# Raw weight pieces in left places, lo parts on VectorE, theta of tiles 0 to 9 in attention: one change to a fused recurrence, mixing and transform kernel

## The chip, the cores and the metric

The kernel runs on one core of one Trainium2 chip. The metric is the device time of one execution in microseconds (us), as the median of several runs. The engines are TensorE (PE in the rows, PEld its weight loads), VectorE (DVE), ScalarE (ACT), GpSimd (POOL) and the SyncE queue that issues most transfers (SP).

## What is computed

Three stages follow one another on 4 batches of 768 tokens with 384 channels (8 heads of 48). The reference, cut to what matters:

```
# 1 attention: a recurrence with decay w and bonus u
cur   = k_t v_t^T * u ;  y_t = r_t (state + cur) ;  state = w_t * state + k_t v_t^T
# 2 mixing over tokens and channels, x is attention's y
theta = x @ w_theta
zr, zi = x * cos(theta), x * sin(theta)
y = w_tok_r @ zr + w_tok_i @ zi          # over the 768 tokens, for every batch
u = x + y ;  x = u + relu(u @ w_ch)
# 3 transform and feed-forward
u = x + real(fft(fft(x, tokens), channels))
out = u + relu(norm(u) @ w_ch1) @ w_ch2
```

The weights arrive as 64-bit floating point numbers, and are made into 32-bit ones on the chip.

## The kernel before

**Weights.** `Feed` loads a weight in pieces of 128 rows. A piece is loaded raw (two 32-bit words for each number, 768 KB for a piece of 768 columns) by `issue`, and `convert` makes one f32 tile of it: ScalarE scales the high words (L496, `prescale`), then VectorE runs three bit operations (L511, L514, L517). There are two raw buffers, so a new raw load can start only when an older piece has been converted. Pieces come in a fixed order: two for w_theta, then twelve for the token weights (w_tok_r and w_tok_i in turn, parts 0 to 11; token tile j needs parts 2j and 2j+1), two for w_ch, and twelve for the feed-forward weights, which go back to DRAM (`store`) after conversion and are read again later. Attention converts the two pieces of w_theta and parts 0 to 5; part 0 goes through DRAM (`tx`), parts 1 to 5 are put into `tst` tiles in the places T19 to T23. The rest is converted in the mixing stage.

**Exact products.** A product of f32 accuracy is made of three matmuls (`mm3`, L445 to L447): each operand is split into a rounded "hi" part and the rest, "lo". The hi part is a copy on ScalarE (L451), the lo part a subtraction (L452) on VectorE or GpSimd, as `split` is told. For the token weights from tile 1 on, for w_ch, and for one of the two z tiles (L651) it is GpSimd before.

**Attention** runs over 16 pairs of heads (i = 0 to 15, four for a batch) in a software pipeline: `front(i)` (transposes L213, products L221, diagonals on ScalarE L228), then `elem` for a later tile on VectorE or some weight conversions (`pieces`: one at i = 1, 5, 9 and 15, two at 13 and 14), then `front2(i)` (copy under a mask L251, L268, the scan L273) and `back(i - 1)` (products L290 and L295, copies of the result out of PSUM L298, stores L305). `THETAS` says at which i the theta matmuls (L433) of which 128-token tiles run in the banks that `back` uses; the result goes to DRAM (L197). At i = 16, which has only a `back`, two more are computed before. Each engine works its instructions off in program order.

**Mixing** (`dense`) is a generator: attention calls `next(nxt)` for its first parts, and the rest follows. It runs over 24 tiles (n = 0 to 23, six for a batch). In loop n TensorE transposes tile n+1 (`tokens`, L610) and then runs the 36 matmuls of tile n (`tok_half`, twice); meanwhile VectorE and ScalarE make tile n+1: turns of theta (L632 to L634), sines (L640, L641), products with x (L646, L647), hi parts (L648, L649) and lo parts (L651, L652). Conversions of pieces are put between these by `side` from the list `work`. Theta of a tile is read back from DRAM if it is in `STORED` or `AHEAD` (`fetch`, L622), else computed in the loop (`angle`). The four tiles of `AHEAD` are computed in loops 0 to 3 and stored. After the sixth tile of a batch come `add_x` and `chan`, the channel product, whose operand u is split by ScalarE and GpSimd. Behind n = 23 follows the last stage, which the change does not touch.

## Time and profile before

| what | value |
|---|---|
| runs | 804.67, 809.67, 808.92 us, median 808.92 us |
| profiled execution | 804.06 us, its span 802.2 us |
| attention | 0 to about 178 us of the span |
| mixing | about 165 to 430 us |
| feed-forward stage | about 430 to 802 us |
| TensorE busy | 744.0 us, 93% |
| VectorE, ScalarE, GpSimd busy | 522.1, 310.7, 173.8 us |

The span runs from the first to the last instruction. Shares are averages over stages with different limits: in the last stage TensorE runs almost without a gap, while around 130 to 265 us it has gaps, and in some of these slices its granted clock is below full speed.

### The profile page before, as it was taken

Reading aid. Unit: us, or ns where it says so; the run is one execution under the profiler, and the core shown is the slowest. Engines: PE = TensorE matmul, PEld = TensorE weight load, DVE = VectorE, ACT = ScalarE, POOL = GpSimd, SP = SyncE. Lnnn points to the kernel's source line nnn. Section 1 sums busy time; section 2 is a strip of 40 time slices with the busy share of each in tenths; the row PEclk is TensorE's granted clock in tenths of the full one; section 3 lists DMA queues with packets and bytes.
Section 4 is the critical chain, followed back from the end, with each engine's and each line's share of the span. In section 5 each row is a group of like instructions: output and inputs, shape, how many; then the busy total and the mean of one; then the engine's idle time right before and its main releaser. Section 6 shows DMA issues by size and latency. Waiting matters only on the chain.

```text
span 802.2 us, 13227 instructions
## 1 busy us (share of the span) xinstructions
PE 744.0 (93%) x5222; PEld 696.5 (87%) x5222; DVE 522.1 (65%) x886; ACT 310.7 (39%) x718; POOL 173.8 (22%) x145
## 2 busy tenths in 40 slices
PE   5699999788598998999999989999999999999996
PEld 4587787567487988999889989999999999999996
DVE  8898997757756875875877796535743476535311
ACT  4487888465334243342333342222322222222110
POOL 2000000005525123224826171004400080000000
PEclk9999999899789999999999999999999999999998
DMA  9878785453323262450452000000010000000101
GB/s 313 232 206 230 209 271 142 163 166 106 98 80 106 79 199 80 128 178 1 139 164 79 1 21 30 20 30 1 21 40 11 31 20 31 20 30 13 38 1 34
DMA packets 35719, 75.46 MB, mean 94 GB/s; under 512 B 5184, under 2 KB 21056, under 8 KB 35264
## 3 DMA queue, kind: packets, MB, share of 16 engines
q1 hardware_dynamic: 34560, 71.24, 29.1%
q0 software_dynamic: 1088, 3.28, 1.2%
q8 instruction: 43, 0.70, 0.4%
q14 instruction: 28, 0.23, 0.1%
HBM read 51.69 MB, written 14.55 MB: 83 GB/s over the span
## 4 chain that ended last, share of the span: by engine, by line
PE 55%; DVE 9%; ACT 3%; issue 3%; DMA 1%; POOL 0%; DVEq 0%; ACTq 0%
PE banks L919 18%; PE banks L446 11%; PE banks L447 11%; PE banks L445 11%; PE banks L433 2%; ACT raw L496 1%; PE banks L854 1%; DVE x L514 1%; DVE ta L633 1%; DMA sq<-sq 1%; DVE z L652 1%; PE banks L893 1%; ACT tmp L641 1%; DVE tmp L646 1%; DVE tmp L647 1%
## 5 line engine op out<-in xcount | busy, mean ns | idle before, releaser
L919 PE MATMUL banks<-W,hb 128*128 128x384 f32 x864 | 167.2, 337 | 0.0
L919 PEld LDWEIGHTS banks<-W,hb 128*128 128x128 f32 x864 | 152.3, 188 | 0.7 <-DVE hb L912 0.6
L912 DVE SCALAR_TENSOR_TENSOR hb<-banks,hb 128x384 fp32r<-128x384 f32 x96 | 53.3, 556 | 96.4 <-ACT hb L911 95.7
L446 PE MATMUL banks<-tok,z 128*128 128x384 f32 x288 | 98.2, 341 | 3.1 <-POOL tok L452 3.1
L911 ACT ACTIVATE hb<-banks 128x384 fp32r<-128x384 f32 x96 | 47.1, 490 | 139.5 <-PE banks L447 139.5
L445 PE MATMUL banks<-un,W 128*128 128x384 f32 x288 | 100.8, 350 | 0.0
L445 PE MATMUL banks<-tok,z 128*128 128x384 f32 x288 | 99.9, 347 | 0.7 <-ACT tok L451 0.7
L447 PE MATMUL banks<-tok,z 128*128 128x384 f32 x288 | 97.9, 340 | 1.2 <-DVE z L652 1.2
L446 PE MATMUL banks<-un,W 128*128 128x384 f32 x288 | 97.5, 339 | 0.2 <-DVE un L452 0.2
L447 PE MATMUL banks<-un,W 128*128 128x384 f32 x288 | 97.4, 338 | 0.0
L651 POOL TENSOR_TENSOR z<-tmp,z 128x384 fp32r<-128x384 f32 x24 | 32.9, 1372 | 279.0 <-DMA sl<-y 165.4
L433 PE MATMUL banks<-wth,sl 128*128 128x384 f32 x144 | 55.9, 529 | 9.1 <-ACT ta L614 5.7
L228 ACT ACTIVATE a<-ident,ktt 128x128 f32<-128x128 f32 x192 | 58.7, 392 | 0.0
L446 PEld LDWEIGHTS banks<-tok,z 128*128 128x128 f32 x288 | 54.9, 190 | 3.9 <-POOL tok L452 3.9
L447 PEld LDWEIGHTS banks<-tok,z 128*128 128x128 f32 x288 | 54.7, 190 | 1.6 <-DVE z L652 1.5
L445 PEld LDWEIGHTS banks<-tok,z 128*128 128x128 f32 x288 | 54.9, 191 | 1.0 <-ACT tok L451 1.0
L446 PEld LDWEIGHTS banks<-un,W 128*128 128x128 f32 x288 | 54.7, 190 | 0.5 <-DVE un L452 0.5
L445 PEld LDWEIGHTS banks<-un,W 128*128 128x128 f32 x288 | 54.9, 191 | 0.0
L447 PEld LDWEIGHTS banks<-un,W 128*128 128x128 f32 x288 | 54.4, 189 | 0.0
L433 PEld LDWEIGHTS banks<-wth,sl 128*128 128x128 f32 x144 | 28.4, 206 | 25.7 <-ACT ta L614 6.3
L640 ACT ACTIVATE tmp<-ta 128x384 f32<-128x384 f32 x24 | 12.6, 523 | 69.8 <-DVE ta L633 63.6
L251 DVE COPY_PREDICATED a<-ktt,banks 128x768 f32<-128x768 uint32 x32 | 31.1, 1013 | 8.3 <-PE banks L221 5.4
(169 smaller groups left out, 1408.0 us busy)
## 6 DMA issues: line engine op xcount, KB each, us to landing
raw<-ch SPq DMA_DIRECT2D x25, 384.0 KB, 4.0
rk<-rk SPq DMA_DIRECT2D x24, 384.0 KB, 5.2
wt<-wt SPq DMA_DIRECT2D x12, 387.5 KB, 4.4
raw<-tok_r SPq DMA_DIRECT2D x6, 768.0 KB, 5.2
raw<-tok_i SPq DMA_DIRECT2D x6, 768.0 KB, 4.5
wx<-x SPq DMA_DIRECT2D x12, 384.0 KB, 5.1
wst<-wx SPq DMA_DIRECT2D x12, 384.0 KB, 3.6
out<-tmp SPq DMA_DIRECT2D x24, 192.0 KB, 2.0
```

The costliest lines, as they stand in the source:

```text
L228: nc.scalar.activation(A[g][:, h, j, :], ident, AF.Copy, scale=aa[:, 3 * g + j, h:h + 1])
L251: nc.vector.copy_predicated(out=asb[i % 2][g], mask=strict.unsqueeze(1).unsqueeze(1).to_broadcast([128, 2, 3, C]), data=pa[g][:, :, 0:3 * ...
L433: nc.tensor.matmul(out, XT[b][:, d, j * 128:(j + 1) * 128], wth[:, d, :], start=d == 0, stop=d == KT - 1)
L445: nc.tensor.matmul(out, ah, bh, start=first, stop=False)
L446: nc.tensor.matmul(out, ah, bl, start=False, stop=False)
L447: nc.tensor.matmul(out, al, bh, start=False, stop=last)
L496: self.nc.scalar.activation(m, m, AF.Copy, scale=REBIAS)
L640: nc.scalar.activation(s, t, AF.Sin, scale=TWOPI)
L651: nc.gpsimd.tensor_tensor(out=z[1][1][j], in0=s, in1=z[1][0][j].bitcast(F32), op=ALU.subtract)
L911: nc.scalar.activation(hh, ph, AF.Relu)
L912: nc.vector.scalar_tensor_tensor(out=hl, in0=ph, scalar=0.0, in1=hh.bitcast(F32), op0=ALU.max, op1=ALU.subtract)
L919: nc.tensor.matmul(po[i], h[hl][:, i * 128:(i + 1) * 128], W[f][k][:, 1, :], start=f == 0 and hl == k == 0, stop=f == nf - 1 and hl == 1)
```

## The change

Five things are changed.

- At i = 12 attention issues two raw pieces more (parts 3 and 4), into the places Z1 and Z0, which `e0` and `e30` of attention have left by then. They don't count as buffers of the feed (`own` is false), so their conversion issues nothing.
- The converted parts 1 to 5 go to the places T21, T22, T23, T19, T20 (`TST`) in this order, before T19 to T23. T18 to T20 hold attention's `wt` tiles, T21 to T23 its `d1`, `dq` and `inc`.
- All lo parts of token weights and w_ch, and both lo parts of z, are made by VectorE. GpSimd keeps the lo parts of u.
- Theta of tiles 0 to 9 runs in attention at i = 6 to 15, one each; nothing at i = 16. `AHEAD` is tiles 10 to 13, its matmuls stand behind tile n = 0 to 3 (before: ahead of it), its copy out of PSUM in the following loop. Tiles 14 to 17 are computed in loops 11 to 14 (before: 14 and 15 at i = 16, 16 and 17 in `AHEAD`, and 4 and 5 in loops 2 and 3).
- Mixing's first `next` is split: at i = 15, ahead of `back(14)`, the token weights of tile 0 are split and part 6 is converted (before: at i = 16, behind z of tile 0; part 6 in loop 0 or 1).

```diff
-THETAS = {6: (0,), 7: (1,), 8: (2,), 9: (3,), 10: (6,), 11: (7,), 12: (8,), 13: (9,), 14: (12,), 15: (13,), 16: (14, 15)}
-AHEAD = (10, 11, 16, 17)
+THETAS = {i + 6: (i,) for i in range(10)}
+AHEAD = (10, 11, 12, 13)
+TST = ("T18", "T21", "T22", "T23", "T19", "T20")
@@ attention, loop over i
+            if i == npair - 1:
+                next(nxt)
             if i == npair - 2:
                 flag()
...
             if i == npair:
                 next(nxt)
-                evict = theta(i)
-                evict(0)
-                evict(1)
             if i >= 1:
                 back(i - 1)
+            if i == npair - 4:
+                for t in ("Z1", "Z0"):
+                    feed.issue(lambda shape, dt, name: pool.tile(shape, dt, name=name, tag=t))
@@ Feed
-    def issue(self):
-        if self.src and len(self.q) < self.bufs:
+    def issue(self, other=None):
+        if self.src and (self.free or other):
             n, parts = self.src.pop(0)
-            raw = self.pool.tile([128, n, 2], U32, name="raw")
+            raw = (other or self.pool.tile)([128, n, 2], U32, name="raw")
+            self.free -= not other
...
-            split(self.nc, y, hi, lo, self.nc.gpsimd)
+            split(self.nc, y, hi, lo)
@@ dense
-                split(nc, ready.pop(0), tok[ri][0][j], tok[ri][1][j], eng)
+                split(nc, ready.pop(0), tok[ri][0][j], tok[ri][1][j])
...
-            nc.gpsimd.tensor_tensor(out=z[1][1][j], in0=s, in1=z[1][0][j].bitcast(F32), op=ALU.subtract)
+            nc.vector.tensor_tensor(out=z[1][1][j], in0=s, in1=z[1][0][j].bitcast(F32), op=ALU.subtract)
...
+        load_tok(0)
+        work += [feed.take(part(6))]
+        side(4)
+        yield
         pt = tokens(0)
...
-            if n < len(AHEAD):
-                t = tmp(2)
-                turned(AHEAD[n], t)
-                nc.sync.dma_start(out=ia["th"][AHEAD[n]], in_=t)
...
+            if 0 < n <= len(AHEAD):
+                t = tmp(2)
+                nc.scalar.activation(t, ahead, AF.Copy, scale=INV2PI)
+                nc.sync.dma_start(out=ia["th"][AHEAD[n - 1]], in_=t)
...
+            if n < len(AHEAD):
+                ahead = theta_mm(nc, bank("q1", [128, DM]), XT, wth, AHEAD[n])
@@ pieces of attention
-            tst[i] = wp.tile([128, S], F32, name="tst", tag=f"T{18 + i}")
+            tst[i] = wp.tile([128, S], F32, name="tst", tag=TST[i])
```

**SP's queue from i = 12 to i = 15** (y is the result of a `back`, th a theta tile on its way to DRAM, raw a weight piece, tst token weights of part 0 read back). Before:

```order
L305 DMA sl_112<-y_1517 48x768 x2
L197 DMA th_90<-th_1578 128x384
L488 DMA raw<-tok_i 128x1536
L488 DMA raw<-tok_r 128x1536
L305 DMA sl_113<-y_1621 48x768 x2
L197 DMA th_91<-th_1682 128x384
L488 DMA raw<-tok_i 128x1536
L488 DMA raw<-tok_r 128x1536
```

and in the changed kernel, up to the read of tst:

```order
L308 DMA sl_110<-y_1515 48x768 x2
L495 DMA raw<-tok_i 128x1536
L495 DMA raw<-tok_r 128x1536
L200 DMA th_90<-th_1580 128x384
L495 DMA raw<-tok_i 128x1536
L495 DMA raw<-tok_r 128x1536
L308 DMA sl_111<-y_1623 48x768 x2
L200 DMA th_91<-th_1684 128x384
...
L200 DMA th_92<-th_1792 128x384
L495 DMA raw<-tok_i 128x1536
L630 DMA ta<-th_83 128x384
L597 DMA tst<-tx 128x768
```

All four raw loads stand one iteration earlier than before; the read of tst stands where it stood, behind the theta store of i = 15 and one raw load.

**ScalarE at the end of attention** (prep of i = 15, y of `back(14)` and `back(15)`, z and tok are hi parts). Before:

```order
L264 ACTIVATE prep_153<-ktt_155 112x48x4
L298 ACTIVATE y_1859<-banks 112x384 x2
L640 ACTIVATE tmp<-ta 128x384
L641 ACTIVATE tmp<-tmp,halfpi 128x384
L648 ACTIVATE z<-tmp 128x384
L649 ACTIVATE z<-tmp 128x384
L451 ACTIVATE tok<-tst 128x768 x2
L196 ACTIVATE th_1915<-banks 128x384
L196 ACTIVATE th_1918<-banks 128x384
L298 ACTIVATE y_1921<-banks 112x384 x2
```

and in the changed kernel:

```order
L267 ACTIVATE prep_151<-ktt_153 112x48x4
L456 ACTIVATE tok<-tst 128x768 x2
L503 ACTIVATE raw<-raw 128x768
L301 ACTIVATE y_1866<-banks 112x384 x2
L648 ACTIVATE tmp<-ta 128x384
L649 ACTIVATE tmp<-tmp,halfpi 128x384
L656 ACTIVATE z<-tmp 128x384
L657 ACTIVATE z<-tmp 128x384
L301 ACTIVATE y_1912<-banks 112x384 x2
```

The hi parts of tst and the scaling of part 6 now stand ahead of the copies of y, and the two theta copies are gone.

**VectorE in loop 2 of mixing**, where two pieces are converted (x), from the products of z on. Before:

```order
L646 TENSOR_TENSOR tmp<-tmp,banks 128x384
L647 TENSOR_TENSOR tmp<-tmp,banks 128x384
L514 SCALAR_TENSOR_TENSOR x<-raw,x 128x768
L517 SCALAR_TENSOR_TENSOR x<-raw,x 128x768
L652 TENSOR_TENSOR z<-tmp,z 128x384
L511 TENSOR_SCALAR x<-raw 128x768
L514 SCALAR_TENSOR_TENSOR x<-raw,x 128x768
L517 SCALAR_TENSOR_TENSOR x<-raw,x 128x768
```

and in the changed kernel:

```order
L654 TENSOR_TENSOR tmp<-tmp,banks 128x384
L655 TENSOR_TENSOR tmp<-tmp,banks 128x384
L521 SCALAR_TENSOR_TENSOR x<-raw,x 128x768
L524 SCALAR_TENSOR_TENSOR x<-raw,x 128x768
L659 TENSOR_TENSOR z<-tmp,z 128x384
L660 TENSOR_TENSOR z<-tmp,z 128x384
L457 TENSOR_TENSOR tok<-x,tok 128x768
L518 TENSOR_SCALAR x<-raw 128x768
L521 SCALAR_TENSOR_TENSOR x<-raw,x 128x768
L524 SCALAR_TENSOR_TENSOR x<-raw,x 128x768
L457 TENSOR_TENSOR tok<-x,tok 128x768
```

One z row and two tok rows (lo parts) came over from GpSimd.

## Rows read from the trace of the kernel before

**Rows 1.** Stretches: length, then busy us of PE, PEld, DVE, ACT, POOL; granted clock; DMA share; GB/s

```profile
130.47:141.57 11.10, 10.45 (x113) 8.22 (x112) 5.74 (x8) 9.05 (x24) 0.00 (x0) 0.85 0.57 144
141.57:158.19 16.62, 11.27 (x116) 8.25 (x115) 13.49 (x24) 7.40 (x20) 0.00 (x0) 0.79 0.43 132
158.19:167.17 8.98, 8.96 (x113) 7.22 (x111) 5.64 (x8) 6.85 (x20) 0.00 (x0) 1.00 0.65 209
167.17:179.21 12.04, 9.43 (x71) 6.30 (x69) 6.33 (x12) 5.75 (x11) 0.99 (x1) 1.00 0.49 157
179.21:250.57 71.36, 56.19 (x267) 47.92 (x265) 50.16 (x60) 30.41 (x52) 31.39 (x18) 0.90 0.34 111
264.45:301.67 37.22, 34.99 (x202) 33.68 (x201) 28.78 (x46) 14.04 (x25) 7.85 (x5) 1.00 0.47 148
317.36:344.46 27.10, 26.88 (x158) 26.49 (x157) 20.46 (x36) 10.25 (x18) 4.71 (x3) 1.00 0.43 127
```

**Rows 2.** Timeline of i = 13, 14: start, duration, instruction, [idle before, releaser]

```profile
141.02 0.56 DVE L511 TENSOR_SCALAR tst<-raw 128x768 uint32<-128x768 uint32 x1 [5.19 <-ACT dm L179]
143.59 0.33 SPq L488 DMA_DIRECT2D raw<-tok_r  x1
147.95 0.92 ACT L496 ACTIVATE raw<-raw 128x768 f32<-128x768 f32 x1 [4.88 <-DMA raw<-tok_r]
145.89 0.80 PE L213 MATMUL banks<-ident,e 112*128 112x112 f32 x4 [2.76 <-DVE pkv L268]
149.29 4.02 PE L433 MATMUL banks<-wth,sl 128*128 128x384 f32 x6 [2.60 <-ACT y L298]
```

**Rows 3.** Timeline from the end of attention to the first tile

```profile
164.81 0.42 SPq L589 DMA_DIRECT2D tst<-tx  x1
169.09 0.36 DVE L632 TENSOR_SCALAR tmp<-ta 128x384 f32<-128x384 f32 x1 [1.80 <-DMA ta<-th]
173.22 1.81 DVE L452 TENSOR_TENSOR tok<-tst,tok 128x768 fp32r<-128x768 f32 x2
174.20 1.52 PE L290 MATMUL banks<-a,v 128*48 128x128 f32 x24 [2.61 <-ACT th L196]
```

**Rows 4.** DMA issues of 384 KB from DRAM: count, KB each, us to landing

```profile
wst<-wx SPq DMA_DIRECT2D x12, 384.0 KB, 3.6
tst<-tx SPq DMA_DIRECT2D x1, 384.0 KB, 7.3
```

**Rows 5.** Groups by shape, 179.2 to 248.8 us: count | busy us, mean ns | idle before

```profile
L517 DVE SCALAR_TENSOR_TENSOR x<-raw,x 128x768 uint32<-128x768 uint32 x7 | 11.0, 1565 | 0.2
L451 ACT ACTIVATE tok<-x 128x768 fp32r<-128x768 f32 x6 | 5.1, 844 | 16.3 <-DVE x L517 16.3
L632 DVE TENSOR_SCALAR tmp<-ta 128x384 f32<-128x384 f32 x5 | 4.7, 936 | 4.1 <-ACT ta L614 4.1
```

**Rows 6.** Groups by shape, 264.4 to 301.7 us (loops 6 to 10)

```profile
L517 DVE SCALAR_TENSOR_TENSOR x<-raw,x 128x768 uint32<-128x768 uint32 x5 | 8.3, 1654 | 0.2
L651 POOL TENSOR_TENSOR z<-tmp,z 128x384 fp32r<-128x384 f32 x5 | 7.9, 1571 | 31.2 <-ACT z L648 31.2
L514 DVE SCALAR_TENSOR_TENSOR x<-raw,x 128x768 uint32<-128x768 uint32 x5 | 4.8, 952 | 0.0
L511 DVE TENSOR_SCALAR x<-raw 128x768 uint32<-128x768 uint32 x5 | 2.8, 561 | 7.8 <-ACT raw L496 7.8
L652 DVE TENSOR_TENSOR z<-tmp,z 128x384 fp32r<-128x384 f32 x5 | 2.7, 546 | 0.0
L632 DVE TENSOR_SCALAR tmp<-ta 128x384 f32<-128x384 f32 x6 | 2.2, 358 | 0.2
```

**Rows 7.** Timeline of mixing: theta, loop 5 on VectorE, channel products

```profile
219.50 4.21 PE L433 MATMUL banks<-wth,sl 128*128 128x384 f32 x6 [5.69 <-ACT ta L614]
244.84 0.35 DVE L632 TENSOR_SCALAR tmp<-ta 128x384 f32<-128x384 f32 x1
250.57 0.44 PE L445 MATMUL banks<-u,wch 128*128 128x384 f32 x1 [1.79 <-ACT u L451]
306.98 0.44 PE L445 MATMUL banks<-u,wch 128*128 128x384 f32 x1 [1.40 <-ACT u L451]
352.83 2.10 PE L433 MATMUL banks<-wth,sl 128*128 128x384 f32 x6
```

More of the change, by code (lines that the diff above doesn't have):

```diff
@@ L488, in issue @@
                 self.nc.sync.dma_start(out=out, in_=src)
-            self.q.append([raw, n, False])
+            self.q.append([raw, n, False, not other])
     def prescale(self, k):
@@ L504, in convert @@
         self.prescale(1)
-        raw, n, _ = self.q.pop(0)
+        raw, n, _, own = self.q.pop(0)
         low, high = raw[:, :, 0], raw[:, :, 1]
@@ L519, in convert @@
         yield
+        self.free += own
         self.issue()
@@ L586, in fetch_tok, with load_tok @@
         def fetch_tok():
[L588 removed]
+            tst[0] = wp.tile([128, S], F32, name="tst", tag=TST[0])
             nc.sync.dma_start(out=tst[0], in_=tx.rearrange("p h n -> p (h n)"))
             ready.extend(tst[i] for i in range(NC))
[L592 removed]
+        def load_tok(j):
             for ri in range(2):
[L594 removed]
+                split(nc, ready.pop(0), tok[ri][0][j], tok[ri][1][j])
         work = []
@@ L943, in dense @@
         fetch(2)
+        held, work[:] = work[:], []
         rotate(0, pt, *sn)
-        load_tok(0, nc.vector)
+        work += held
         yield
@@ L952, in dense @@
                 fetch(last[0] + 2)
-            if n < len(AHEAD):
-                t = tmp(2)
-                turned(AHEAD[n], t)
-                nc.sync.dma_start(out=ia["th"][AHEAD[n]], in_=t)
             if n <= 4:
-                work += [feed.take(part(i)) for i in ((6, 7), (8,), (9, 10), (11,), (12, 13))[n]]
+                work += [feed.take(part(i)) for i in ((7,), (8,), (9, 10), (11,), (12, 13))[n]]
             if n in conv:
```

4 lines of the change are left out of this document (1 added, 3 removed).

## The prediction

> **What bounds the kernel now.** I first read the table of stretches. In the last stage nothing changes, so the question is where the stretches from 130 to 350 us lose time. An iteration of attention takes 8.98 us when nothing disturbs it (i = 15), but i = 14 takes 16.62 us, with TensorE busy for 11.27 of them and a granted clock of 0.79 [rows 1]. From the last iteration to the first matmul of tile 0 go 12.04 us, and tiles 0 to 5, up to the first channel product, take 71.36 us with 56.19 us of TensorE work [rows 1]. In loops 6 to 10 the clock is 1.00 and TensorE still has small gaps: five loops take 37.22 us, 7.44 each [rows 1]. In loops 12 to 15 TensorE is busy for 26.88 of 27.10 us, so there it is the bound [rows 1].
>
> Then the timelines, for what ends last. At i = 13 VectorE stands still for 5.19 us before L511: the second piece of that iteration goes into the place of a `wt` tile that ScalarE's last `dm` still reads [rows 2]. So the piece's raw buffer comes free late, the raw load goes out at 143.59, and ScalarE waits 4.88 us for it at 147.95 [rows 2]. Behind this wait stand the copies of y, and TensorE waits twice, 2.76 us for VectorE's late L268 and 2.60 us for y [rows 2].
>
> In tiles 0 to 5 VectorE's operations are longer than elsewhere: L517 1565 ns, L632 936 ns on the mean, against 952 ns for L514, which is of the same shape, and 358 ns for L632 in loops 6 to 10 [rows 5, 6]. There too L517 takes 1654 ns, always while GpSimd's z operation of 1571 ns runs [rows 6]. So GpSimd's operations are paid for by VectorE; without them L517 should cost what L514 does.
>
> **Step 1, i = 14.** Parts 1 to 5 no longer go into places of `wt` that are still read, and parts 3 and 4 are loaded at i = 12. Both waits of [rows 2] end. VectorE's work of i = 14 fits into about 9 us (two conversions of 0.56 + 2 x 0.95 us [rows 6] make 5), so I give it i = 15's length, 9.0 us in place of 16.62: -7.6. It could be as long as i = 13, 11.10 (clock 0.85) [rows 1]: -5.5; that it is shorter than i = 15 nothing speaks for. The two loads more at i = 12 stand in SP's queue ahead of a theta store only, and the total loaded by i = 15 is the same.
>
> **Step 2, from attention to tile 0.** Two theta tiles and one of `AHEAD` leave this place on TensorE, but they were not all of the path. The order now puts the hi parts of tst ahead of ScalarE's copies of `back(14)`. tst is read behind the theta store of i = 15 and a raw load, as before; it was issued at 164.81 and took 7.3 us [rows 3, 4], so it landed at 172.1, and nobody waited. Shifted by step 1 it lands at 164.5, and now ScalarE waits for it, with y, L290 and z of tile 0 behind it. After landing: two hi parts (0.84 each, [rows 5]) and the second lo part (0.9, half of [rows 3]'s 1.81) 2.6 us; conversion of part 6 2.5; z of tile 0 as before, from 169.09 to 173.22 [rows 3], less about 0.2 as the new z part fits into a wait, 3.9. z stands at 164.5 + 9.0 = 173.5. The other 384 KB reads from DRAM take 3.6 us [rows 4]; with that, everything here comes 3.7 earlier.
>
> **Step 3, loops 0 to 5.** VectorE becomes the bound. A loop with one conversion takes 7.44 us before; L517 falls by 0.70 (1.65 to 0.95) and the second z part adds 0.55 [rows 6]: 7.3. To this come the lo parts, 0.9 each, and waits of about 0.9 for the hi part where it stands right behind its conversion:
> loop 0: 7.3 + 4 x 0.9 + two such waits (0.7 and 0.9) = 12.5;
> loop 1: 7.3 + 3 x 0.9 = 10.0;
> loop 2: 7.3 + 0.9 + a second conversion 2.5 + 0.9 + 0.9 = 12.5;
> loop 3: 7.3 + 0.9 = 8.2;
> loop 4: 7.3 + 0.9 + a conversion of half width 1.8, its lo part 0.6 and wait 0.9 = 11.5.
> Together 54.7, so loop 5 starts on VectorE at 228.2 (before: 244.84, [rows 7]). From there to the channel product it was 5.73 us (250.57, [rows 7]); with the second z part 6.3: 234.5. TensorE's own work in loops 0 to 4 is 5 tiles of 6.6 us (26.49 / 4, [rows 1]) and 4 thetas of 1.95 (2.10 less the tail that overlaps, [rows 7]), 41 us, and stays below. So steps 1 to 3 give 234.5 in place of 250.57: -16.1. Bounds: without the waits behind conversions (4 x 0.9) -19.7; with every L517 and L632 as long as in [rows 5], 7 x 0.6 + 5 x 0.58 = 7.1 more, -9.0.
>
> A rule speaks against this move. The Trainium skill (Perfetto Trace Analysis, Optimizing Scalar/DVE Operations) says that where VectorE is saturated, giving work to ScalarE or even GpSimd may help, though hardly between VectorE and GpSimd as they share a read port. By its first half the moved parts would be a plain loss: 0.55 us for a z part, 0.9 for a tok part. By the row a z part on GpSimd costs VectorE 0.70, so moving it gains 0.15 a loop; the caveat of its second half is what the trace shows.
>
> **Step 4, the rest.** TensorE will stand idle for some 4 us ahead of the channel product of loop 5 (before 1.79, [rows 7]), and after an idle time of 5.69 the three theta matmuls took 4.21 us in place of 2.10 [rows 7]: +1 (0 to +2). Loops 6 to 10: 5 x -0.15, then +0.5 at each of two channel products: 0. Theta of 14 falls into the wait ahead of the channel product of loop 11 (1.40 at least, [rows 7]): 0. Theta of 15, 16 and 17 falls into loops 12 to 14, where TensorE has no room: 3 x 1.95 less the 0.22 idle and some 0.3 of rounding, +5.3 (+3.2 if VectorE's 7.44 were the bound there and 8.53 = 6.6 + 1.95 the new length, +5.8 at most). Loops 17 to 23 have no conversions or slack enough: 0 to +2, I take 0.
>
> **Sum.** -16.1 + 1 + 0 + 5.3 = -9.8, made against the profiled execution's 804.06: 794.3. That execution lies at the lower end of the runs (804.67 to 809.67, median 808.92); I add half of the distance to the median, 2.4: **796.7 us**.
>
> **Rivals.**
> *tst comes early.* With 3.6 us of transfer, as wst has it, -13.5: 793.0. For it: the queue is emptier at i = 14 and 15. Against: the raw load right ahead of it is the same.
> *Step 1 gives nothing:* the waits at i = 14 stay, as transfers now, since four raw loads of 768 KB go out within some 6 us. Then -9.8 + 7.6 = -2.2: 804.3. Against: the row waits for a load issued only 4.4 us before, and the new ones go out an iteration, 9 to 11 us, before they are needed.
> *VectorE stays as slow without GpSimd.* Then L517 and L632 keep their lengths: +7.1 in loops 0 to 4 and 0.70 in five loops more, +3.5, together +0.8: 807.3, no change. Against: in [rows 6] L514 of the same shape takes 952 ns, beside no GpSimd work.
> *TensorE's clock, the one that ends slower.* With VectorE as the bound, TensorE waits 2 to 4 us in every loop from 0 to 5. If it came back at 1.2 GHz each time and stayed there, its work from tile 0 to the end of that channel product, 6 x 6.6 + 4 x 1.95 + 9.9 (54 matmuls at a tile's 6.6 us for 36) = 57 us, would take 114: 40 more than the forecast's 73 with waits, 837. It is slower than before once more than 12 us come back this way. For it speaks that the stretch of loops 0 to 5 already has 0.90, and the row of 5.69 idle [rows 1, 7]; against it, that with such waits the mean stayed at 0.90. The Trainium skill (TensorE: Matmul & The Clock Gate, HAM oscillation) describes such loops, which start cold in every round; the trace agrees for single waits, and no run here shows it for every loop.
>
> **Chances.** The forecast 0.65, tst early 0.12, step 1 nothing 0.12, VectorE as slow 0.06, the clock 0.05. The forecast's own spread is some 7 us either way, from the bounds of steps 1, 3 and 4 (789 to 804). The range is 787 to 806: it takes in the first two rivals. About 1% (8 us) is what a measurement of this kernel can tell from no change, so faster means below 800.8. Of the forecast 0.55 and all of tst early lie there, faster 0.67; same 0.27; slower 0.06.
>
> **What would show it.** Step 1: in the changed kernel i = 14 takes 9 us, with no wait for a raw load. Step 2: ScalarE's tok<-tst waits some 5 us for a DMA, and L290 of `back(15)` behind it for y. Step 3: L524 at 0.95 us, loops of 12.5, 10, 12.5, 8 and 11.5 us on VectorE, TensorE idle in each. Step 4: loops 12 to 14 at 8.5 us. I am wrong if TensorE's clock is below 0.8 in loops 0 to 5, if VectorE waits for raw loads there, or if lo parts on VectorE take much more than 0.55 and 0.9 us.

## The result and the profile after

The changed kernel takes 783.12 us (median of 4 runs, 782.83 to 785.0) against 806.79 for the kernel before (median of 4, 803.41 to 809.67) on the same chip. The ratio is 0.9713, with a 95% interval of 0.9665 to 0.9761. Forecast were 796.7 us with a range of 787 to 806: the direction is right, but the time is 13.6 us below the forecast and lies below the range. The profiled execution of the changed kernel took 783.26 us, its span 781.5 (before 804.06 and 802.2).

The busy time by engine (share of the span, instructions):

```profile
PE 738.4 (94%) x5222; PEld 694.4 (89%) x5222; DVE 514.0 (66%) x922; ACT 311.0 (40%) x718; POOL 118.0 (15%) x109
```

VectorE has 36 instructions more than before and is busy for 514.0 us in place of 522.1. GpSimd loses 36 instructions and 55.8 us. So the moved operations cost VectorE less than what GpSimd had cost it.

The stretches that answer to [rows 1]. Columns: start and end, length, busy us of PE, PEld, DVE, ACT, POOL, granted clock, DMA share, GB/s. They are i = 13, i = 14, i = 15, from there to the transposes of tile 1 (right ahead of tile 0's matmuls), from there to the first channel product, five loops behind it, and the loops with theta of tiles 15 to 17:

```profile
131.92:140.80 8.88, 8.88 (x114) 7.30 (x112) 8.64 (x13) 8.85 (x25) 0.00 (x0) 1.00 0.84 219
140.80:151.20 10.40, 9.15 (x115) 7.31 (x114) 9.59 (x19) 8.54 (x22) 0.00 (x0) 1.00 0.64 242
151.20:159.92 8.72, 8.72 (x112) 7.19 (x112) 5.82 (x9) 5.44 (x17) 0.00 (x0) 1.00 0.45 140
159.92:170.84 10.92, 5.11 (x50) 4.21 (x48) 6.50 (x11) 4.68 (x9) 0.00 (x0) 0.69 0.41 125
170.84:229.39 58.55, 52.16 (x261) 46.05 (x261) 47.16 (x80) 29.94 (x52) 0.00 (x0) 0.94 0.43 144
242.81:278.89 36.08, 34.99 (x204) 33.98 (x203) 27.63 (x52) 14.05 (x25) 0.00 (x0) 1.00 0.46 148
294.25:326.54 32.29, 32.29 (x176) 29.76 (x174) 21.57 (x40) 12.73 (x23) 0.00 (x0) 1.00 0.36 110
```

i = 14 falls from 16.62 to 10.40 us, and i = 13 from 11.10 to 8.88 at full clock. The stretch up to the channel product of loop 5 falls from 71.36 to 58.55 us, and five loops behind it from 37.22 to 36.08. The last row is longer than its answer before, since these thetas now lie in it. Behind i = 15 the clock falls to 0.69 in the changed kernel, where TensorE waits for y; this holds back L293 (2.80 us in place of 1.52 [rows 3]), but not z of tile 0 on VectorE.

The timelines of i = 14 and of the end of attention, which answer to [rows 2, 3] (start, duration, instruction, in brackets the idle time before it and what ended it):

```profile
142.61 0.98 ACT L503 ACTIVATE raw<-raw 128x768 f32<-128x768 f32 x1 [1.03 <-DMA raw<-tok_r]
144.02 2.20 PE L438 MATMUL banks<-wth,sl 128*128 128x384 f32 x6 [1.22 <-ACT y L301]
157.46 0.42 SPq L597 DMA_DIRECT2D tst<-tx  x1
163.05 1.58 ACT L456 ACTIVATE tok<-tst 128x768 fp32r<-128x768 f32 x2 [5.13 <-DMA tst<-tx]
165.85 2.80 PE L293 MATMUL banks<-a,v 128*48 128x128 f32 x24 [5.38 <-ACT y L301]
171.97 0.36 DVE L640 TENSOR_SCALAR tmp<-ta 128x384 f32<-128x384 f32 x1
```

The waits of 5.19 and 4.88 us of [rows 2] are gone; 1.03 us for a raw load stays. ScalarE now waits 5.13 us for tst, and TensorE behind it for y, as forecast. tst landed 5.6 us after its issue (before 7.3 [rows 4]).

The groups of VectorE's operations from 171.9 to 224.6 us, which answer to [rows 5] (count | busy us, mean ns | idle before):

```profile
L524 DVE SCALAR_TENSOR_TENSOR x<-raw,x 128x768 uint32<-128x768 uint32 x6 | 5.7, 958 | 0.2
L457 DVE TENSOR_TENSOR tok<-x,tok 128x768 fp32r<-128x768 f32 x6 | 5.7, 958 | 3.2 <-ACT tok L456 3.2
L660 DVE TENSOR_TENSOR z<-tmp,z 128x384 fp32r<-128x384 f32 x6 | 3.3, 553 | 0.0
L640 DVE TENSOR_SCALAR tmp<-ta 128x384 f32<-128x384 f32 x6 | 2.1, 354 | 0.0
```

L524 is the old L517 (1565 ns before), L640 the old L632 (936 ns before). Both have their undisturbed durations.

Where the 20.7 us of the span went, by the starts of the same work in the two traces (TensorE's first instruction, but VectorE's L632 or L640 for the start of loop 5):

| stretch | before | after | change | forecast |
|---|---|---|---|---|
| start to i = 13 | 130.47 | 131.92 | +1.5 | 0 |
| i = 13 to 15 | 36.70 | 28.00 | -8.7 | -7.6 |
| from there to loop 5 | 77.67 | 64.58 | -13.1 | -9.0 |
| loop 5 to its channel product | 5.73 | 4.89 | -0.8 | +0.6 |
| channel product of loop 5 | 11.95 | 11.96 | 0.0 | +1 |
| loops 6 to 11 | 54.84 | 52.90 | -1.9 | 0 |
| loops 12 to 17 | 55.38 | 60.74 | +5.4 | +5.3 |
| loop 18 to the end | 429.46 | 426.51 | -3.0 | 0 |
| sum | 802.2 | 781.5 | -20.7 | -9.8 |

The first part of the program takes its own time in each execution. In the profiles shown here i = 12 starts between 121.67 and 126.59 us, although the same amount of work runs before it in all. So kernels are compared below also by the time from the start of i = 12 to the end of the span: 680.5 us before, 658.3 after. These are the first transposes of i = 12 in the timeline of TensorE, before and after:

```profile
121.68 0.31 PE L213 MATMUL banks<-ident,e 112*128 112x112 f32 x1
```

```profile
123.21 0.31 PE L216 MATMUL banks<-ident,e 112*128 112x112 f32 x1
```

### The profile page after: what moved, and what is told of

Read it like the earlier page. It is cut to its first block, busy times and chain, and to the rows that moved or that the text cites. A ratio compares the mean times of both kernels' runs of the same rounds, so it can differ in the third digit from the quotient of the medians.

```text
span 781.5 us, 13205 instructions
## 1 busy us (share of the span) xinstructions
PE 738.4 (94%) x5222; PEld 694.4 (89%) x5222; DVE 514.0 (66%) x922; ACT 311.0 (40%) x718; POOL 118.0 (15%) x109
## 4 chain that ended last, share of the span: by engine, by line
PE 69%; issue 14%; DVE 12%; ACT 3%; DMA 1%; POOL 1%; SPq 0%; DVEq 0%; ACTq 0%; POOLq 0%
PE banks L927 19%; PE banks L451 12%; PE banks L452 12%; PE banks L450 12%; PE banks L438 4%; PE banks L224 2%; PE banks L293 1%; DVE a L254 1%; PE banks L862 1%; DVE q L161 1%; PE banks L298 1%; PE banks L901 1%; PE banks L236 1%; DVE inc L150 1%; PE banks L216 1%
## 5 line engine op out<-in xcount | busy, mean ns | idle before, releaser
L457 POOL TENSOR_TENSOR u<-sl,u 128x384 fp32r<-128x384 f32 x24 | 24.0, 1016 | 338.2 <-ACT u L456 338.2
L451 PEld LDWEIGHTS banks<-tok,z 128*128 128x128 f32 x288 | 54.3, 189 | 0.0
```

Source lines behind the costliest of these rows:

```text
L451: nc.tensor.matmul(out, ah, bl, start=False, stop=False)
L457: (eng or nc.vector).tensor_tensor(out=lo, in0=src, in1=hi.bitcast(F32), op=ALU.subtract)
```

## The experiments

Ratios are to the kernel before, run on the same chip beside each group. "From i = 12" is the time from the start of i = 12 to the end of the profiled span.

| run | kernel | median us | ratio, 95% interval | from i = 12 |
|---|---|---|---|---|
| e1 | before + places | 803.67 | 0.9978 (0.9963 to 0.9992) | 680.4 |
| e2 | before + raw loads | 801.52 | 0.9961 (0.9945 to 0.9977) | 676.0 |
| e3 | before + both | 800.54 | 0.9937 (0.9914 to 0.9959) | 676.9 |
| e13 | the same again | 798.42 | 0.9923 (0.9881 to 0.9964) | 673.1 |
| e4 | before + lo parts on VectorE | 791.29 | 0.9842 (0.9808 to 0.9875) | 666.5 |
| e5 | after, z part on GpSimd | 793.84 | 0.9833 (0.9774 to 0.9892) | 670.3 |
| e14 | the same again | 791.61 | 0.9851 (0.9818 to 0.9884) | 664.7 |
| e6 | after, all lo parts on GpSimd | 794.76 | 0.9851 (0.9795 to 0.9907) | 667.9 |
| e7 | after, old tables of theta | 786.70 | 0.9762 (0.9705 to 0.9818) | 660.3 |
| e8 | after, late split | 784.29 | 0.9722 (0.9665 to 0.9779) | 657.1 |
| e9 | after again | 787.75 | 0.9782 (0.9736 to 0.9827) | 658.4 |
| e10 | after, tst read early | 781.38 | 0.9707 (0.9663 to 0.9752) | 653.5 |
| e11 | after, theta of eight tiles early | 779.84 | 0.9694 (0.9646 to 0.9743) | 654.7 |
| e12 | after, both of these | 778.16 | 0.9647 (0.9601 to 0.9692) | 649.6 |

The changed kernel's second set of runs (e9) came 4.6 us above the first, yet from i = 12 the two profiles agree within 0.2 us: the difference in the profile lies ahead of i = 12, at 126.48 in place of 123.21.

### Which part of the first step removes the waits at i = 13 and 14

e1 is the kernel before with the new places alone:

```diff
+TST = ("T18", "T21", "T22", "T23", "T19", "T20")
...
-            tst[0] = wp.tile([128, S], F32, name="tst", tag="T18")
+            tst[0] = wp.tile([128, S], F32, name="tst", tag=TST[0])
...
-            tst[i] = wp.tile([128, S], F32, name="tst", tag=f"T{18 + i}")
+            tst[i] = wp.tile([128, S], F32, name="tst", tag=TST[i])
```

> The kernel before with the converted parts in the places T18, T21, T22, T23, T19, T20 and nothing else changed. Theory A, the place is the whole cause: VectorE's wait of 5.19 us at i = 13 goes, the raw buffers come free some 5 us earlier, the raw loads land in time and i = 14 falls from 16.62 to 9 to 11 us; 798 to 801 us in all against the 804 to 809 of the kernel before. Theory B, with two raw buffers the loads of parts 3 and 4 still come too late: a wait of 2 us or more for a raw load stays at i = 14, which takes 13 us or more, and the time is 803 to 806 us. I expect A.

ScalarE's timeline at i = 14 of e1:

```profile
144.50 0.91 ACT L499 ACTIVATE raw<-raw 128x768 f32<-128x768 f32 x1 [1.16 <-DMA raw<-tok_i]
147.80 0.88 ACT L499 ACTIVATE raw<-raw 128x768 f32<-128x768 f32 x1 [2.40 <-DMA raw<-tok_r]
```

VectorE's wait for `dm` is gone, but ScalarE still waits 1.16 and 2.40 us for raw loads. i = 14 takes 15.46 us, only 1.2 less than before, and the median is 0.9 us lower (the profiled execution, 806.16, is the slowest of the ten). Theory B holds, and what I expected was wrong.

e2 is the kernel before with the raw loads alone (`...` stands for the edit of `Feed`, as in the change):

```diff
+            if i == npair - 4:
+                for t in ("Z1", "Z0"):
+                    feed.issue(lambda shape, dt, name: pool.tile(shape, dt, name=name, tag=t))
...
```

> The kernel before with the two raw loads at i = 12 into Z1 and Z0 and nothing else changed. The places of the converted parts are still read by ScalarE's dm, so VectorE's wait at i = 13 stays near 5 us. Theory A, the place is the cause and the raw load only follows from it: the wait of 4.88 us for the raw load goes, but the iteration still carries the late VectorE work: i = 13 and i = 14 together 23 to 26 us (27.7 before, 19.3 in the changed kernel), 802 to 806 us in all. Theory B, the raw load is the cause: the two together below 21 us and 798 to 801 us.

VectorE's timeline at i = 13 of e2:

```profile
142.87 0.56 DVE L515 TENSOR_SCALAR tst<-raw 128x768 uint32<-128x768 uint32 x1 [5.30 <-ACT dm L179]
```

Here the other wait stays, 5.30 us for ScalarE's `dm`, while the wait for the raw load is gone. i = 13 and 14 together take 24.73 us (27.72 before), inside theory A's 23 to 26; the time is 0.5 us below its 802 to 806. So neither edit alone takes both waits away, but they don't give equally little: the raw loads alone shorten i = 13 and 14 by 3.0 us and the median by 3.1.

e3 has both edits, on the kernel before.

> The kernel before with the new places and the two raw loads at i = 12, nothing else. If these two make the whole gain up to the end of attention (i = 13 to i = 15 went from 36.7 to 28.0 us in the changed kernel), the three iterations take 28 to 29 us here too and the time is 796 to 800 us. If the thetas that left i = 13 to 16 took part in it (the theta at i = 13 takes 3.32 us before and 2.15 after), i = 13 stays at 10 to 11 us and the time is 799 to 802 us.

The stretches i = 12 to 14 of e3 (columns as above); i = 15 takes 8.71 us:

```profile
123.51:132.82 9.31, 8.87 (x113) 7.26 (x111) 9.11 (x12) 7.55 (x23) 0.00 (x0) 1.00 0.57 157
132.82:142.34 9.52, 8.88 (x113) 7.26 (x111) 9.28 (x12) 9.03 (x25) 0.00 (x0) 1.00 0.83 219
142.34:155.30 12.96, 11.90 (x116) 8.91 (x115) 10.29 (x21) 8.60 (x22) 0.00 (x0) 0.74 0.49 183
```

i = 13 to 15 take 31.2 us here, against 28.0 in the changed kernel. The waits are nearly the same as there (0.94 us of ScalarE for a raw load, 1.06 of TensorE for y); 2.6 of the 3.2 us lie at i = 14, where the granted clock is 0.74. Neither of the two expected cases came. e5, which has all of the change but the z part, showed it too (0.74 at i = 14, 12.89 us). So e3 and e5 were run again.

> The kernel before with the new places and the two raw loads once more. In the first profile i = 12 to 14 took 9.31, 9.52 and 12.96 us with a granted clock of 0.74 at i = 14; the changed kernel, which differs there in no wait, took 8.71, 8.88 and 10.40 at full clock. If this is a matter of the execution, a profile with 8.7, 8.9 and 10.3 is as likely as one with a low clock, and the time then lies some 4 us below a cold one. If the thetas or the conversions of the kernel before make it, the three lengths come again within 0.3 us.

i = 12 to 14 of e13, where i = 15 takes 8.72 us:

```profile
121.87:130.59 8.72, 8.72 (x114) 7.19 (x113) 8.51 (x11) 7.57 (x23) 0.00 (x0) 1.00 0.46 108
130.59:141.39 10.80, 10.56 (x113) 8.16 (x111) 9.90 (x14) 9.38 (x25) 0.00 (x0) 0.84 0.87 250
141.39:150.90 9.51, 8.90 (x115) 7.29 (x113) 9.06 (x19) 8.05 (x22) 0.00 (x0) 1.00 0.50 185
```

The same kernel now has the lower clock at i = 13 instead (0.84), and i = 13 to 15 take 29.0 us. The three lengths did not come again. e12, another kernel with both edits, shows the e13 pattern (10.83 and 9.52), and e6 to e8 and e14 show that of the changed kernel (8.9 and 10.3). So the lengths of i = 12 to 14 belong to the execution, within some 4 us. The two edits together are worth 7.4 us from i = 12 in e13 and 3.6 in e3; the forecast for them was 7.6. By the medians, which take in several executions, they are worth 4.1 us in e3 (804.60 to 800.54) and 5.6 in e13 (804.06 to 798.42).

### What VectorE gains when GpSimd stops

e4 is the kernel before with the lo parts on VectorE and nothing else:

```diff
-            split(self.nc, y, hi, lo, self.nc.gpsimd)
+            split(self.nc, y, hi, lo)
...
-                split(nc, ready.pop(0), tok[ri][0][j], tok[ri][1][j], eng)
+                split(nc, ready.pop(0), tok[ri][0][j], tok[ri][1][j])
...
-            nc.gpsimd.tensor_tensor(out=z[1][1][j], ...)
+            nc.vector.tensor_tensor(out=z[1][1][j], ...)
```

> The kernel before with all lo parts of token weights, w_ch and z on VectorE, nothing else. The stretch from z of tile 0 (173.2) to the channel product of loop 5 (250.6) is 77.3 us before and 57.5 in the changed kernel. Theory A, GpSimd's operations beside VectorE's are what makes this stretch long: L517 falls from 1.57 to 0.95 us and L632 from 0.94 to 0.36, and the stretch falls by 6 us or more; 795 to 800 us in all. Theory B, the added parts (about 8 at 0.9 us and 5 at 0.55 us, some 10 us) take back what the shorter operations give (7 x 0.6 and 5 x 0.58, 7 us, and 0.7 in five loops): the stretch stays within 3 us of 77 and the time within 3 us of the kernel before; the gain of the changed kernel would then lie in the order of conversions and thetas.

This edit alone gives 13.3 us of the medians and 14.0 us from i = 12: theory A, and more than it said. VectorE's loops 0 to 4 fall from 69.9 to 62.5 us, loops 6 to 11 from 54.8 to 52.9. Another 1.7 us is the channel product's clock, 1.00 in this profile and 0.88 before (from the transposes of tile 7 to those of tile 8).

What GpSimd costs VectorE is seen in VectorE's groups from 175 to 244.8 us in the kernel before, beside those of [rows 5]:

```profile
L514 DVE SCALAR_TENSOR_TENSOR x<-raw,x 128x768 uint32<-128x768 uint32 x7 | 8.3, 1189 | 0.1
L511 DVE TENSOR_SCALAR x<-raw 128x768 uint32<-128x768 uint32 x7 | 5.7, 821 | 13.6 <-ACT raw L496 12.3 <-issue 1.3
L652 DVE TENSOR_TENSOR z<-tmp,z 128x384 fp32r<-128x384 f32 x5 | 4.3, 868 | 0.0
L633 DVE TENSOR_TENSOR ta<-ta,tmp 128x384 f32<-128x384 f32 x5 | 4.3, 858 | 0.2
```

Against their undisturbed durations [rows 6] (L514 0.95, L511 0.56, L652 0.55; L633 took 0.56 in the loops 6 to 10) these lose 7 x 0.24 + 7 x 0.26 + 5 x 0.32 + 5 x 0.30 = 6.6 us. L517 and L632 lose 7 x 0.61 + 5 x 0.58 = 7.2 us. The prediction knew the second sum alone.

The timelines of GpSimd (first fence) and of VectorE (second) in loop 1 of the kernel before show how:

```profile
200.08 4.61 POOL L452 TENSOR_TENSOR tok<-tst,tok 128x768 fp32r<-128x768 f32 x2
204.65 1.93 POOL L452 TENSOR_TENSOR tok<-x,tok 128x768 fp32r<-128x768 f32 x1
```

```profile
200.86 2.15 DVE L652 TENSOR_TENSOR z<-tmp,z 128x384 fp32r<-128x384 f32 x1
203.05 1.85 DVE L632 TENSOR_SCALAR tmp<-ta 128x384 f32<-128x384 f32 x1
204.94 2.06 DVE L633 TENSOR_TENSOR ta<-ta,tmp 128x384 f32<-128x384 f32 x1
207.03 0.36 DVE L634 TENSOR_SCALAR tmp<-ta 128x384 uint32<-128x384 uint32 x1
```

These three VectorE operations start while GpSimd works, and each ends only behind the GpSimd operation that then runs: they take 2.15, 1.85 and 2.06 us in place of 0.55, 0.36 and 0.56. L634, which starts behind GpSimd's last one, takes 0.36. The Trainium skill (SBUF — State Buffer, Who interferes with whom) says that VectorE shares one pair of ports with GpSimd, that operations with two SBUF inputs and those in a two-port mode need it, and that the holder keeps it for the whole instruction. These rows agree for L652 and L633, and for L632 if it runs in such a mode. Not every VectorE operation is slowed. L672 reads one operand from PSUM and one from SBUF, and its six operations ahead of the channel product (minimum, median and maximum in ns) keep their length, though GpSimd works from 250.60 on:

```profile
L672 DVE TENSOR_TENSOR sl<-banks,sl x6: 540/540/544, 249.4 to 251.7; 128x384 f32<-128x384 f32 x6
```

The 13.8 us that VectorE's operations lost are not the gain of loops 0 to 4, for the moved operations are added there. VectorE in these loops (length, its busy us, granted clock, DMA share, GB/s), before and in e4:

```profile
174.96:244.84 69.88, 46.64 (x55) 0.90 0.32 104
175.10:237.61 62.51, 44.15 (x72) 0.95 0.35 116
```

With 17 operations more VectorE is busy for 2.5 us less; the other 4.9 of the 7.4 us are shorter waits. Its wait for ScalarE's scaling of a raw piece ahead of L511 falls from 12.3 to 8.7 us, that for theta from 4.1 to 1.6, and 2.2 us of idle time for which the profile shows no releaser go, while 3.3 us of waits for hi parts come. VectorE was not saturated here before, as it stood idle for a third of the time. Which of these waits became shorter because VectorE's operations did, and which because the lo parts came earlier, no run separates.

e6 and e5 undo the move in the changed kernel, e6 all of it and e5 the z part alone (the edit of e5):

```diff
-            nc.vector.tensor_tensor(out=z[1][1][j], ...)
+            nc.gpsimd.tensor_tensor(out=z[1][1][j], ...)
```

> The changed kernel with all lo parts where the kernel before has them: token weights from tile 1 on, w_ch and one z part on GpSimd. Theory A, moving them to VectorE is the larger part of what was gained from 172 to 250 us: VectorE's five loops 0 to 4 go from 52.5 to 60 us or more, and the time is 793 to 799 us. Theory B, the move is worth little there, and the order of theta and of conversions is what was gained: loops 0 to 4 at 51 to 55 us, and the time 784 to 789 us, the rest from loops 6 to 11 and the end.

> The changed kernel with the one z lo part back on GpSimd, the lo parts of token weights and w_ch still on VectorE. The changed kernel stands at 783.1 us. Theory A, GpSimd's z operation costs VectorE more than the 0.55 us that it saves it: loops 6 to 11 go from 52.9 back to some 54.8 us, loops 0 to 4 get longer by 0.5 to 1 us each, the end of the mixing stage by 1 to 3 us: 786 to 790 us. Theory B, the shorter loops 6 to 11 and the shorter end have another cause: 782 to 784.5 us with loops 6 to 11 at 53 us.

e6 is 9.6 us slower than the changed kernel from i = 12: VectorE's loops 0 to 4 take 56.9 us in place of 52.5, loops 6 to 11 take 54.9 in place of 52.9, and some 1 to 2 us come in the end of the span. Of the 4.4 us in loops 0 to 4, 3.5 are busy time of VectorE (45.1 us in place of 41.6). Its time of 794.76 lies inside theory A's 793 to 799, but the loops fell between the two theories. e5's 793.84 was above what either theory said. Its profiled execution, the slowest of its four (797.99), holds the low clock at i = 14 and 0.78 around the channel product. Run again:

> The changed kernel with the one z lo part on GpSimd once more. In the first profile 3.7 us of its 12 us over the changed kernel lay at i = 12 to 14 (12.89 us and a clock of 0.74 at i = 14), where no z is made, and 2.1 us in the channel product of loop 5 (clock 0.78). If both belong to the execution, i = 14 takes some 10.3 us this time, the rest stays (loops 0 to 4 at 54.3 us, loops 6 to 11 at 54.9) and the time is 789 to 793 us; if they belong to the kernel, they come again and the time is 792 to 797 us.

i = 14 takes 10.25 us this time, and the kernel is 6.3 us slower than the changed one from i = 12. Loops 0 to 4 take 54.3 us (+1.8) and loops 6 to 11 take 54.8 (+1.9), both as in e5, and 791.61 us is inside the first case's range. So the z part makes some two thirds of the 9.6 us, and the lo parts of the weights the rest. In the tail, loops 18 to 22 follow the z part: they take 26.1 us in all kernels that have it on GpSimd and 25.7 in all others. The last stage alone (from tile 23's transposes) doesn't: it takes 400.3 to 402.0 us among kernels that have the lo parts on VectorE, and 401.9 in e14 and e6.

The loops 6 to 11 show the exchange in clean form. VectorE in a loop of the kernel before, from L514 to the start of the next loop:

```profile
283.63 0.95 DVE L514 SCALAR_TENSOR_TENSOR x<-raw,x 128x768 uint32<-128x768 uint32 x1
284.61 1.66 DVE L517 SCALAR_TENSOR_TENSOR x<-raw,x 128x768 uint32<-128x768 uint32 x1
286.19 0.54 DVE L652 TENSOR_TENSOR z<-tmp,z 128x384 fp32r<-128x384 f32 x1
286.77 0.36 DVE L632 TENSOR_SCALAR tmp<-ta 128x384 f32<-128x384 f32 x1
```

and of the changed kernel:

```profile
261.54 0.95 DVE L521 SCALAR_TENSOR_TENSOR x<-raw,x 128x768 uint32<-128x768 uint32 x1
262.52 0.96 DVE L524 SCALAR_TENSOR_TENSOR x<-raw,x 128x768 uint32<-128x768 uint32 x1
263.40 0.55 DVE L659 TENSOR_TENSOR z<-tmp,z 128x384 fp32r<-128x384 f32 x1
263.87 0.55 DVE L660 TENSOR_TENSOR z<-tmp,z 128x384 fp32r<-128x384 f32 x1
264.45 0.36 DVE L640 TENSOR_SCALAR tmp<-ta 128x384 f32<-128x384 f32 x1
```

From L517 to L652 it was 1.58 us, from L524 to L659 it is 0.88: 0.70 gained. The second z part moves what follows by 0.47 (263.40 to 263.87), not by its duration of 0.55, since consecutive operations overlap by 0.08. The loop is 0.23 us shorter: 7.22 in place of 7.45.

### What the theta tables and the early split are worth

e7 is the changed kernel with the old tables:

```diff
-THETAS = {i + 6: (i,) for i in range(10)}
-AHEAD = (10, 11, 12, 13)
+THETAS = {6: (0,), 7: (1,), 8: (2,), 9: (3,), 10: (6,), 11: (7,), 12: (8,), 13: (9,), 14: (12,), 15: (13,), 16: (14, 15)}
+AHEAD = (10, 11, 16, 17)
...
             if i == npair:
                 next(nxt)
+                evict = theta(i)
+                evict(0)
+                evict(1)
```

> The changed kernel with the old tables THETAS and AHEAD, so that tiles 14 and 15 are again at i = 16, 16 and 17 in AHEAD (still behind the tile's matmuls), 4 and 5 in loops 2 and 3. Theory A, the new tables only move work from a stretch where TensorE waits to one where it is full: loops 12 to 14 get 5.3 us shorter, and tile 0 starts no later since ScalarE waits for tst there anyway: 777 to 780 us. Theory B, the two thetas at i = 16 (some 4 us) and the two in loops 2 and 3 (2 to 4 us) stand in the way of VectorE's loops: 782 to 787 us.

It is 2.0 us slower than the changed kernel from i = 12. Loops 12 to 17 get 5.8 us shorter (54.92 in place of 60.74), but VectorE's loops 0 to 4 take 60.2 us in place of 52.5: VectorE waits 4.52 us at the start of loop 4 for theta of tile 5, which is computed in loop 3 behind TensorE's matmuls:

```profile
222.09 0.36 DVE L643 TENSOR_SCALAR tmp<-ta 128x384 f32<-128x384 f32 x1 [4.52 <-ACT ta L625]
```

Part of the difference is hidden by the clock of the channel product, which was full in this profile; without it the tables are worth some 3.5 us. The median of 786.7 lies in theory B's range, though not by enough that the times alone would tell it from 783.1 and 787.75.

e8 is the changed kernel with the late split:

```diff
-        load_tok(0)
-        work += [feed.take(part(6))]
-        side(4)
         yield
         pt = tokens(0)
...
         rotate(0, pt, *sn)
+        load_tok(0)
...
-            for i in ((7,), (8,), (9, 10), (11,), (12, 13))[n]
+            for i in ((6, 7), (8,), (9, 10), (11,), (12, 13))[n]
```

> The changed kernel with the token weights of tile 0 split behind z of tile 0, and part 6 in loop 0, as before. Theory A, the read of tst on which ScalarE waits 5.13 us is on the path: with the copies of y and z of tile 0 ahead of it they come some 4 us earlier, the wait is filled, and the time is 779 to 782 us. Theory B, the work of VectorE is what counts and part 6 (2.5 us) is better done where VectorE waits in attention: loop 0 gets 2.5 to 4 us longer and the time is 784 to 787 us.

Both in part: VectorE's loop 0 starts 4.4 us earlier, as theory A said, and is 3.5 us longer, as theory B said. 784.29 us lies at the edge of theory B's range, but it is no difference that can be told from the changed kernel, and the 1.2 us that are left from i = 12 are less than what the channel product's clock gives (11.59 in place of 13.42 us between two transposes). The early split moves 2.5 us of VectorE's work to a place where ScalarE's wait for tst then holds back the rest.

### What is left to gain

e9 is the changed kernel again, for the three others of its group.

> The changed kernel once more, so that the three below are compared with it on one chip: 783 us, 0.971 of the kernel before.

e10 reads tst at i = 13:

```diff
+            if i == npair - 3:
+                read_tst()
...
-            tst[0] = wp.tile([128, S], F32, name="tst", tag=TST[0])
-            nc.sync.dma_start(out=tst[0], in_=tx.rearrange("p h n -> p (h n)"))
+            if 0 not in tst:
+                read_tst()
```

> The changed kernel with the read of tst issued at i = 13 in place of i = 15, ahead of the theta store, the raw load and the reads of theta behind which it stands. Theory A, the late read is on the path to tile 0: ScalarE's wait of 5.13 us goes; behind it stands only the raw load of part 6, issued at 156.4, which should land at 160 to 162, so the copies of y come 2 to 4 us earlier and the time is 779 to 781 us. Theory B, the start of tile 0 is set by VectorE or by the raw load as late: 782.5 to 784 us.

SP's read of tst and ScalarE's first hi part in e10:

```profile
146.10 0.58 SPq L1157 DMA_DIRECT2D tst<-tx  x1
158.82 1.57 ACT L458 ACTIVATE tok<-tst 128x768 fp32r<-128x768 f32 x2
161.63 1.52 PE L293 MATMUL banks<-a,v 128*48 128x128 f32 x24 [0.16 <-ACT y L301]
```

The median is 781.38 us, 6.4 below e9 and 0.4 above theory A's range. The wait for tst is gone, and TensorE's wait for y falls from 5.38 to 0.16 us. From the end of i = 15 to VectorE's loop 0 it takes 7.98 us in place of 12.05. From i = 12 the kernel is 4.8 us shorter, some 1.6 of it the channel product's clock. So the late read was on the path, as step 2 said.

e11 computes theta of tiles 14 to 17 in loops 0, 1, 2 and 4:

```diff
-AHEAD = (10, 11, 12, 13)
+AHEAD = tuple(range(10, 18))
+HALF = {0: 14, 1: 15, 2: 16, 4: 17}
...
+                if n in HALF:
+                    t = tmp(2)
+                    turned(HALF[n], t)
+                    nc.sync.dma_start(out=ia["th"][HALF[n]], in_=t)
                 tok_half(b, j, 1, ...)
...
```

> The changed kernel with theta of tiles 14 to 17 also computed in loops 0, 1, 2 and 4, between the two halves of the tile's matmuls, where TensorE waits for VectorE, and no longer in loops 11 to 14. If the 5.3 us that loops 12 to 14 took more are TensorE's alone, they go, and loops 0 to 4 have 52.5 us for 5 x 6.6 + 8 x 1.95 = 48.6 us of work: 777.5 to 780 us. If TensorE becomes the bound in loops 0 to 4, since its waits there do not lie where the work is, 4 us or more come back: 782 to 785 us.

The median is 779.84 us, and from i = 12 the kernel is 3.6 us shorter than the changed one. Loops 12 to 17 give back 5.8 us (54.94). VectorE's loops 0 to 4 take 54.8 us, 2.3 more, and wait that long for TensorE; from loop 5 to the channel product it takes 7.0 us, 2.2 more, and TensorE reaches the channel product without a gap. So the time lies in the first case's range, but 4.4 us come back, as the second case said. In exchange the channel product, which has full clock here, is 2.5 us shorter (9.48 in place of 11.95).

> The early read of tst and theta of tiles 14 to 17 in loops 0, 1, 2 and 4 together. If the two gains add up: 774 to 777.5 us. If an earlier tile 0 leaves TensorE less time for the thetas: no better than the better one of the two.

Both together: 778.16 us, ratio 0.9647 (0.9601 to 0.9692) against 0.9782 (0.9736 to 0.9827) of the changed kernel on the same chip, and 8.8 us less from i = 12. From i = 12 the two gains add up (4.8 and 3.6), though each of the three holds a channel product at full clock (1.5 to 2.5 us). By the medians they don't: e10 is 6.4 us below e9, e11 7.9, and e12 9.6. So how far they add up is not shown. The 774 to 777.5 expected was 0.7 us too low, against a changed kernel that came 4.7 above its expected time in this group. e12 has the lowest median here.

## Why the prediction was right and wrong

**Where the miss lies.** By the table the profile came out 10.9 us below the sum. Step 4 was too high by 5.8 us (channel product 1.0, loops 6 to 11 1.9, the end 3.0, theta 0.1 the other way), step 3 by 3.6, step 2 by 1.9 and step 1 by 1.1; the start was 1.5 us longer. 2.4 us more are the addition for the median, and the rest is rounding. The mechanisms of steps 1 to 3 were right, and what failed there are the sizes. The step that failed most is step 4: the loops 6 to 11 and the end were put at 0 and gave 1.9 and 3.0 us.

**Step 1 was right in mechanism, and in size partly by luck.** Forecast were 9.0 us for i = 14 and -7.6. i = 14 took 10.40 (-6.2), and the sum of i = 13 to 15 came to -8.7 since i = 13, which I had left at its length, fell by 2.2. The same two edits on the kernel before gave 5.5 us there in e3 and 7.7 in e13, and 4.1 and 5.6 us of the medians. e1 and e2 show that the row of 5.19 and the row of 4.88 in [rows 2] are two waits with two releasers: the place, and the number of raw buffers. The claim that the raw load goes out late because of the place is only half of it; with the place mended it is still too late by 2.40 us. The wait of 1.03 us that stays at i = 14 was not forecast: I had the load go out 9 to 11 us before it is needed, and it went out 6.5 us before (136.06 to 142.61).

**Step 2 was right, its transfer too long.** ScalarE's wait, y and L290 (now L293) behind it came as written, and from the landing of tst to z of tile 0 it took 8.9 us against 9.0 forecast. tst took 5.6 us, between the two rows of [rows 4], of which I had taken the 7.3 for the value. This was 1.7 us; in e9, the same kernel, tst took 6.4, so about half of it belongs to the execution. e10 confirms that the read was on the path.

**Step 3 was right in mechanism and failed in its sizes, by 3.6 us.** VectorE and the ScalarE operations that it waits for set the length of loops 0 to 4 (41.6 us of the 52.5 busy, the rest waits for ScalarE's scaled pieces, hi parts and sines, none for theta), and the order of the loop lengths was right: 11.74, 9.72, 12.42, 8.01 and 10.64 us against 12.5, 10.0, 12.5, 8.2 and 11.5. TensorE did not stand idle in each loop, which I had named as a sign: it has two gaps, 2.31 and 3.10 us. Each length was too long, together by 2.2 us, since the loop without extra work is 7.22 and not 7.3, one of loop 0's waits replaces another, and the half-width wait is 0.59 in place of 0.9. From loop 5 to the channel product it was 1.4 us too long again: I had added the second z part to the 5.73 us of before, but e4, which has the move alone, takes 4.88 us there too, so the move shortens this stretch.

The rule weighed there (the Trainium skill, Perfetto Trace Analysis, Optimizing Scalar/DVE Operations) would by its first half have had the move cost time. e4 shows 13.3 us of gain from it alone, and e6 9.6 us of loss from i = 12 when it is undone. The rule speaks of a saturated VectorE, which this was not (46.64 of 69.88 us busy). I knew the price of GpSimd's work by L517, and in the bounds and the rival by L632 too; L511, L514, L633 and L652 paid nearly as much (6.6 us against 7.2). This made the bound and the rival too small, but not the forecast of loops 0 to 4, which was added up from undisturbed rows.

**Step 4 failed by the most: three small terms were all too high.** The loops 6 to 11 gave 1.9 us where I had put nothing: 0.23 a loop in place of 0.15, as the second z part costs the distance between starts (0.47) and not its duration (0.55), and the 0.5 that I took back at each channel product did not come. The clock cost nothing more than before: TensorE stood idle for 0.97 us ahead of the channel product, not for the 4 that I had reckoned with. The kernel before had already paid it there (first row), and the changed one pays the same (second):

```profile
250.57:262.52 11.95, 11.31 (x54) 11.03 (x55) 6.63 (x12) 4.37 (x9) 7.10 (x7) 0.86 0.07 18
```

```profile
229.39:241.35 11.96, 11.32 (x55) 11.03 (x56) 7.20 (x14) 4.41 (x9) 6.08 (x6) 0.86 0.06 16
```

The prediction's rows did not hold the clock of this stretch. The end of the span gave 3.0 us, where I had allowed for 0 to +2 and taken 0 without a row for it. 0.4 of it lie in loops 18 to 22, where they go with the z part (26.1 to 25.7 us). In the last stage, 0.6 us is a wait of TensorE for VectorE in the waits from 398 to 440 us of the kernel before (first of the rows below), which is absent in the changed kernel, and 0.9 are waits of matmuls for the load of sq, a constant of the last stage (the other two rows; in the changed kernel 0.3, of a weight load). That the load is late because GpSimd's queue issues it behind the z operations is not borne out: in both kernels it goes out when TensorE leaves its place, and the slower of its two halves took 8.2 us in e4, without GpSimd's z work, and 5.8 in e5, with it. The rest of the 3.0 is not settled.

```profile
PE banks L445 <- DVE eb L452: 0.6, 1, 0.6
PE banks L447 <- DMA sq<-sq: 0.6, 1, 0.6
PE banks L445 <- DMA sq<-sq: 0.3, 1, 0.3
```

Theta of tiles 14 to 17 was right to a tenth, +5.4 against +5.3, and the loops give it back in e11.

**The 2.4 us from the profile to the median were wrong.** They were added to the sum as half of the distance to the runs' median; the changed kernel's median lies at its profile. e9 shows that a set of runs can as well lie 4.6 us higher.

**The rivals.** That tst comes early held by half (1.7 of 3.7 us). Step 1 giving nothing, and VectorE staying slow, did not happen. That e6 is 9.6 us slower, near the 10.6 of the second of these, bears out no price: in e6 the moved operations are off VectorE as well, and the rival had them on it. The clock's rival did not happen: in VectorE's loops 0 to 4 the granted clock is 0.94, and TensorE's waits of 2.3 to 3.1 us were followed by thetas of 3.16 and 3.61 us in place of 2.10. The range was too narrow downward since I let the errors of the terms cancel, while nearly all had one sign: losses that I assumed, or gains that I left out, without a row that shows them in the new order.

## What to carry to other kernels

Where GpSimd works beside a VectorE on whose chain the others wait, add up what all of VectorE's operations lose in the stretches where GpSimd is busy, not only the one that stands out; it can be more than the work itself costs on VectorE. Look at each kind of operation: here L672, with an operand in PSUM, lost nothing. Count the waits as well, which in e4 were two thirds of the gain in loops 0 to 4. Price an operation that is added to a chain by the distance between starts in the trace, not by its duration. A wait that is removed may have a second one with another releaser behind it, as here the place and the number of buffers. Neither edit alone removed both waits, though the raw loads alone brought 3.1 of the 4.1 us of the medians (e2, e3). A term that is put at nothing needs a row as much as any other: here two such terms made 4.9 of the 13.6 us of the miss.
